# Second batch, first two groups: layer-norm statistics by ScalarE accumulators instead of VectorE batch-norm instructions

## The chip, the cores and the metric

The kernel runs on one core of a Trainium2 chip. The metric is the device time of one launch in microseconds (us). Over three runs the kernel before took 1139.4 us in the median (1138.05 to 1140.47). A core has five engines with a queue each, and each works through its queue strictly in order: PE (TensorE, matmuls), DVE (VectorE), ACT (ScalarE), POOL (GpSimd) and SP (SyncE, which here only starts DMAs). They wait for one another through semaphores.

## The reference, cut to what matters

For 8 batches of 4224 positions with 192 channels the reference computes a dynamic convolution and feeds its output `x` to a Fourier-mixing block with an MLP:

```
w   = softmax(weight_gen)                      # 7 taps, 8 heads
x   = sum over k of w[k] * x_padded[s + k]     # convolution, per head
X   = real(fft over channels(fft over positions(x)))
u   = x + X
mu  = mean(u, axis=-1);  var = mean((u - mu)**2, axis=-1)
un  = (u - mu) / sqrt(var + 1e-6)
out = u + max(un @ w_ch1, 0) @ w_ch2           # 192 -> 768 -> 192
```

The change concerns only how `mu` and `var` are obtained for two pieces of one batch. What is computed stays the same.

## The kernel before, in words

**Tiling.** The 4224 positions of a batch lie as 128 partitions by 33 rows. The rows form nine groups per batch, eight of four rows (128x4x192) and one of a single row; group 1,0 below means batch 1 (the second), group 0. With 8 batches the MLP runs over 72 groups, numbered n = 9b + g.

**Stages of a batch b.**
- `conv(b)`: softmax of the taps on DVE and ACT (L279 to L286), then per group c seven products on DVE (L441), the first into the tile `u`, six into tiles `pr`, which POOL adds to `u` (L450; from batch 2 on all six). A fold on POOL (L464, L466), a first Fourier stage on PE (`pg`, L471), copies on ACT (L476, L478) and sums on DVE (L480, L482) give `gt`, which SP writes to a DRAM buffer `g_d` (L485, L486).
- `transform(b)`: SP reads `g_d` back (L507) in another layout when the whole convolution is done; PE makes the second Fourier stage (`pp`, L517), ACT copies it to `pq` (L521 to L531).
- `mix(b, g)`: third stage on PE (`eo`, L546), an ACT copy (`ot`, L551), four DVE sums into `u` (L552 to L556). `u` is then the input of the norm.
- `norm(b, g)`: statistics, `rs` (row 0: 1/sigma, row 1: the bias -mu/sigma), normalisation on ACT (`un`, L601), a split into two 16-bit halves `hl` (ACT L609, POOL L610 and L612), and a transposing DMA into `ht` (L618).
- `mlp(n)`: PE multiplies `ht` with the first weight in six pieces of five matmuls (`ph`, L643); ACT takes the relu as a 16-bit tile `hh` (L653), DVE the rest that the 16 bits lose (L654, from group 7 on); PE multiplies both with the second weight for the group before (`po`, L666); DVE adds into `u` (L671), SP stores it (L675). `ph` has three buffers, `po` two, the product tiles `pr` five, `un` one.

**Two ways to the statistics.** The flag `quick` in `norm` (L571) chooses. With it, DVE runs four BN_STATS and four BN_AGGR (L580, L581), ACT one square root (L582), DVE the reciprocal (L593) and four small products for the bias (L596). Without it, ACT makes four sums (L586) and four sums of squares (L590) with its accumulator, between them one scaling (L588), then the root (L592); DVE makes the reciprocal (L593), and from batch 1 on POOL the bias in one small product (L599). Before the change `quick` holds for groups 0 to 2 of batch 0 and for groups 0 and 1 of batch 1.

**What sets the order.** `run()` steps generators by due times that are written in units of groups, so that the convolution of batch b+1 runs beside the MLP of batch b. The tile framework then places the instructions of each engine's queue with its own timing model of the whole program (`schedule_with_timeline_sim=True`, L812). So an edit in one place can move instructions everywhere behind it.

Of the kernel before, what the change touches and what calls it, by code (L numbers as in the profile page):

```python
# [30 lines left out]
QUICK = 3  # L31
# [61 lines left out]
def tile_dynconv_fnet_mlp(  # L93
# [20 lines left out]
    NG = 9  # L114
# [6 lines left out]
    def pst(tag, bufs, shape, dt, name):  # L121
        return ps.tile(shape, dt, tag=tag, name=name, bufs=bufs)
# [367 lines left out]
    def keep_warm(bank, nm, lhsT, rhs, count):  # L490

        spare = pst(*bank, [P, 512], F32, f"warm_{nm}")
        for _ in range(count):
            nc.tensor.matmul(spare[:, 0:rhs.shape[-1]], lhsT=lhsT, rhs=rhs, start=True, stop=True)
# [69 lines left out]
    def norm(b, g):  # L564

        T = min(4, N2 - 4 * g)
        u = uv = us[b, g]
        st = sb.tile([P, 4, 2], F32, tag="st", name=f"st_{b}_{g}", bufs=2)
        rs = sb.tile([P, 3, 4], F32, tag="rs", name=f"rs_{b}_{g}", bufs=2)
        junk = sb.tile([P, D], F16, tag="junk", name=f"junk_{b}_{g}", bufs=2)  # L570
        quick = NG * b + g < QUICK or (b == 1 and g < 2)  # L571
        if NG * b + g < QUICK:
            halves = [pst("ph", 3, [P, 2, D], F32, f"un_{b}_{g}_{i}") for i in range(2)]
        else:
            un = sb.tile([P, 4, D], F32, tag="un", name=f"un_{b}_{g}", bufs=1)
            halves = [un[:, 0:2], un[:, 2:4]]
        if quick:
            bn = sb.tile([P, 4, 6], F32, tag="bn", name=f"bn_{b}_{g}", bufs=2)
            for t in range(T):
                nc.vector.bn_stats(out=bn[:, t, :], in_=uv[:, t, :])  # L580
                last_bn[b, g] = nc.vector.bn_aggr(out=st[:, t, :], in_=bn[:, t, :])  # L581
            nc.scalar.activation(rs[:, 0, 0:T], st[:, 0:T, 1], AF.Sqrt, bias=eps_t)  # L582
            neg = -1.0
        else:
            for t in range(T):
                nc.scalar.activation(junk, uv[:, t, :], AF.Identity, accum_out=st[:, t, 0:1])  # L586
            neg = -1.0 / D
            nc.scalar.mul(rs[:, 2, 0:T], st[:, 0:T, 0], neg)  # L588
            for t in range(T):
                nc.scalar.activation(junk, uv[:, t, :], AF.Square, bias=rs[:, 2, t:t + 1],  # L590
                                     accum_out=st[:, t, 1:2])
            nc.scalar.activation(rs[:, 0, 0:T], st[:, 0:T, 1], AF.Sqrt, bias=eps_t, scale=1.0 / D)  # L592
        nc.vector.reciprocal(out=rs[:, 0, 0:T], in_=rs[:, 0, 0:T])  # L593
        if quick or b == 0:
            for t in range(T):
                nc.vector.tensor_scalar(out=rs[:, 1, t:t + 1], in0=st[:, t, 0:1], scalar1=rs[:, 0, t:t + 1],  # L596
                                        scalar2=neg, op0=ALU.mult, op1=ALU.mult)
        else:
            nc.gpsimd.tensor_tensor(out=rs[:, 1, 0:T], in0=rs[:, 2, 0:T], in1=rs[:, 0, 0:T], op=ALU.mult)  # L599
        for t in range(T):  # L600
            nc.scalar.activation(halves[t // 2][:, t % 2, :], uv[:, t, :], AF.Identity,  # L601
                                 bias=rs[:, 1, t:t + 1], scale=rs[:, 0, t:t + 1])
        yield 0.5
        warm = NG * b + g == 0
        hl = sb.tile([P, 4, 2 * D], F16, tag="hl", name=f"hl_{b}_{g}", bufs=2)
        lo_eng = nc.vector if NG * b + g < QUICK else nc.gpsimd
        spans = [(un, 0, T)] if NG * b + g >= QUICK else [(h, 2 * i, 2 * i + 2) for i, h in enumerate(halves)]
        for src, t0, t1 in spans:
            nc.scalar.copy(hl[:, t0:t1, 0:D], src[:, 0:t1 - t0, :])  # L609
            lo_eng.tensor_tensor(out=hl[:, t0:t1, 2 * P:3 * P], in0=src[:, 0:t1 - t0, 0:P],  # L610
                                 in1=hl[:, t0:t1, 0:P], op=ALU.subtract)
            last_lo[NG * b + g] = lo_eng.tensor_tensor(out=hl[:, t0:t1, D:2 * P], in0=src[:, 0:t1 - t0, P:D],  # L612
                                                       in1=hl[:, t0:t1, P:D], op=ALU.subtract)
        if warm:
            keep_warm(("ph", 3), f"hl{g}", hl[:, 0, 0:P], hl[:, T - 1, 0:2 * D], WARM[2])
        hls[NG * b + g] = hl
        ht = sb.tile([P, 4, 3, P], F16, tag="ht", name=f"ht_{b}_{g}", bufs=3)
        nc.sync.dma_start(ht[:, 0:T].rearrange("p t q m -> p (t q) m"),  # L618
                          hl[:, 0:T, :].rearrange("p t d -> p (t d)"), transpose=True)
        state[b, g] = (us.pop((b, g)), ht)  # L620
        yield 2.0
# [110 lines left out]
    for g in range(QUICK):  # L732
        add(0.0, 1.0, behind(last_split[-1].ins, mix(0, g)))
        run()
        add(0.0, 1.0, norm(0, g))
        run()
# [33 lines left out]
    for b in range(B):  # L770
        t0 = NG * b
        pp_at, mix_at, step = (NG - HELD + 0.6, NG - HELD, 0.6) if b == 1 else (PP_AT, 3.0, MIX_STEP)
        if b > 0:
            add(free_at, t0 - pp_at - (CONV_LEAD if b > 1 else 0), next_conv(b) if b > 1 else rest())
            add(t0 - pp_at, t0 - mix_at, transform(b))
            free_at = t0 - pp_at
        for g in range(NG):
            if b > 0 or g >= QUICK:
                at = t0 - mix_at + step * g + (0.7 if b == 0 else 0)
                add(at, at + step, late_mix(g) if b == 0 and g >= QUICK else mix(b, g))  # L780
                add(max(at + step, t0 + g - 2.0), t0 + g - 1.0, norm(b, g))
# [38 lines left out]
```

## Time and profile before

| | |
|---|---|
| median of three runs | 1139.4 us (1138.05 to 1140.47) |
| the profiled execution: its time | 1140.4 us |
| its span, first to last instruction | 1138.5 us, 23781 instructions |
| busy shares of the span | PE 95%, DVE 85%, POOL 76%, ACT 71% |
| granted PE clock | 0.99 on average |

So 1.9 us of the execution's time lie outside the span, and this execution is 1.0 us above the median. A row of a timeline gives start, duration, engine, line, operation and tiles, and in square brackets how long the engine idled before it and for what. Rows of groups give the total busy time and the mean of one in ns. PE overlaps its matmuls: a row of several lasts longer than its share of the queue, so starts are compared with starts.

### The profile page before, as it was taken

The numbers are of one execution on the slowest core, as the hardware profiler recorded it, in microseconds if no ns is written. First come the engines' busy times: TensorE is split into PE (matmuls) and PEld (weight loads), VectorE is DVE, ScalarE is ACT, GpSimd is POOL, SyncE is SP. The second block draws the span as 40 slices with busy tenths as digits, with TensorE's granted clock in tenths as the row PEclk, the third lists the DMA queues.
The fourth block names the chain that finished last, engine by engine and source line by source line (L and its number), as shares of the span: only waits on it lengthen the run. The fifth ranks groups of instructions, "written<-read, shape, count | busy, mean of one in ns | idle before, by whom it ended". The sixth has DMA issues, their size and how long they took to land.

```text
span 1138.5 us, 23781 instructions
## 1 busy us (share of the span) xinstructions
PE 1077.6 (95%) x8476; PEld 816.1 (72%) x8476; DVE 971.3 (85%) x1821; ACT 810.2 (71%) x2522; POOL 867.2 (76%) x745
## 2 busy tenths in 40 slices
PE   5985999998999999999989999999999999999998
PEld 3454677786777867777768867777777867887777
DVE  7988999989989998999988998999899996356443
ACT  4666775456975899569864898668975898579822
POOL 4979598699969998799959998699969998011200
PEclk9996999999999999999999999999999999999999
DMA  8354245514573348415742357415562234422321
GB/s 299 133 150 111 51 115 138 167 39 123 115 205 85 94 115 207 115 50 129 200 117 67 105 106 206 126 39 125 153 144 58 71 73 98 115 56 48 85 46 47
DMA packets 156504, 128.74 MB, mean 113 GB/s; under 512 B 108571, under 2 KB 133088, under 8 KB 156384
## 3 DMA queue, kind: packets, MB, share of 16 engines
q1 hardware_dynamic: 156384, 127.21, 42.1%
q8 instruction: 67, 1.10, 0.4%
q14 instruction: 53, 0.43, 0.1%
HBM read 61.46 MB, written 39.37 MB: 89 GB/s over the span
## 4 chain that ended last, share of the span: by engine, by line
PE 51%; DVE 14%; POOL 11%; ACT 8%; issue 8%; DMA 6%; SPq 1%; POOLq 0%; DVEq 0%; ACTq 0%
PE ph L643 21%; PE po L666 18%; POOL u L450 8%; PE pp L517 5%; DVE pr L441 5%; PE eo L546 2%; DMA g<-g_d 2%; DMA g_d<-gt 2%; PE pa L446 2%; PE pg L471 2%; DVE hh L654 1%; ACT junk L590 1%; DMA ht<-hl 1%; ACT junk L586 1%; ACT hh L653 1%
## 5 line engine op out<-in xcount | busy, mean ns | idle before, releaser
L450 POOL TENSOR_TENSOR u<-u,pr 128x768 f32<-128x768 f32 (+1 forms) x390 | 645.5, 1679 | 63.1 <-DVE pr L441 43.6
L666 PEld LDWEIGHTS <-hh 128*128 128x128 f16 x4248 | 365.1, 99 | 77.2 <-DVE hh L654 5.5
L666 PE MATMUL po<-w2h,hh 128*128 128x192 f16 x2832 | 416.0, 246 | 4.2 <-DVE hh L654 4.1
L643 PE MATMUL ph<-ht,w1h 128*128 128x512 f16 (+1 forms) x1296 | 394.0, 362 | 7.1 <-DMA ht<-hl 3.9
L441 DVE TENSOR_TENSOR pr<-x_sb,wp 128x768 f32<-128x768 f32 (+1 forms) x415 | 354.0, 875 | 17.5 <-POOL u L450 13.3
L666 PE MATMUL po<-w2l,hh 128*128 128x192 f16 x1416 | 345.4, 246 | 0.0
L654 DVE SCALAR_TENSOR_TENSOR hh<-ph,hh 128x512 f16<-128x512 f32 (+1 forms) x390 | 244.8, 634 | 103.2 <-ACT hh L653 101.5
L643 PE MATMUL ph<-ht,w1l 128*128 128x512 f16 (+1 forms) x864 | 309.8, 362 | 0.0
L653 ACT ACTIVATE hh<-ph 128x512 f16<-128x512 f32 (+1 forms) x390 | 213.7, 550 | 129.8 <-PE ph L643 103.6
L643 PEld LDWEIGHTS <-w1h 128*128 128x128 f16 x1296 | 125.5, 98 | 94.7 <-DMA ht<-hl 3.2
L601 ACT ACTIVATE un<-u,rs 128x192 f32<-128x192 f32 x264 | 123.7, 536 | 24.5 <-DVE rs L596 7.9
L610 POOL TENSOR_TENSOR hl<-un,hl 128x512 f16<-128x512 f32 (+1 forms) x69 | 75.6, 1096 | 70.5 <-ACT hl L609 32.4
L643 PEld LDWEIGHTS <-w1l 128*128 128x128 f16 x864 | 85.0, 98 | 52.6 <-issue 4.0
L590 ACT ACTIVATE junk<-u,rs 128x192 f16<-128x192 f32 x244 | 110.6, 453 | 3.2
L586 ACT ACTIVATE junk<-u 128x192 f16<-128x192 f32 x244 | 88.1, 361 | 21.9 <-DVE u L556 19.2
L546 PE MATMUL eo<-cs_sb,pq 97*128 97x97 f32 x544 | 84.5, 273 | 3.5 <-DVE u L556 2.9
L521 ACT COPY pq<-pp 97x204 f32<-97x204 f32 (+1 forms) x96 | 46.7, 488 | 56.9 <-PE pp L517 56.3
L546 PEld LDWEIGHTS eo<-cs_sb,pq 97*128 97x128 f32 x544 | 77.3, 191 | 10.6 <-issue 5.2
L671 DVE SCALAR_TENSOR_TENSOR u<-po,isc,u 128x384 f32<-128x384 f32 (+1 forms) x122 | 72.5, 594 | 8.5 <-PE po L666 8.3
L464 POOL TENSOR_TENSOR sm<-u 128x382 f32<-128x382 f32 x64 | 65.6, 1025 | 5.8 <-DMA g_d<-gt 2.7
L666 PE MATMUL po<-w2f,hh 128*128 128x192 f32 x336 | 62.3, 327 | 0.0
L599 POOL TENSOR_TENSOR rs<-rs 128x4 f32<-128x4 f32 (+1 forms) x61 | 12.8, 213 | 61.5 <-ACT hh L653 37.8
(110 smaller groups left out, 1316.9 us busy)
## 6 DMA issues: line engine op xcount, KB each, us to landing
out_dram<-u SPq DMA_DIRECT2D x64, 384.0 KB
x_sb<-in_x_dram SPq DMA_DIRECT2D x48, 384.0 KB
g<-g_d SPq DMA_DIRECT2D x40, 336.0 KB
x_sb<-in_x_dram SPq DMA_DIRECT2D x8, 864.0 KB
g_d<-gt SPq DMA_DIRECT2D x32, 195.0 KB
g_d<-gt SPq DMA_DIRECT2D x32, 189.0 KB
w<-in_weight_gen_dram SPq DMA_DIRECT2D x6, 924.0 KB
x_sb<-in_x_dram SPq DMA_DIRECT2D x8, 672.0 KB
```

Source lines behind the costliest of these rows:

```text
L441: last_product[b] = nc.vector.tensor_tensor(out=dst, in0=rows, in1=wk, op=ALU.mult)
L450: adder.tensor_tensor(out=u, in0=u, in1=pr, op=ALU.add)
L546: nc.tensor.matmul(eo[:, e, j, :], lhsT=pq[0:DH, e, r, r:r + P], rhs=cs_sb[:, e, :], start=True, stop=True)
L586: nc.scalar.activation(junk, uv[:, t, :], AF.Identity, accum_out=st[:, t, 0:1])
L590: nc.scalar.activation(junk, uv[:, t, :], AF.Square, bias=rs[:, 2, t:t + 1], accum_out=st[:, t, 1:2])
L601: nc.scalar.activation(halves[t // 2][:, t % 2, :], uv[:, t, :], AF.Identity, bias=rs[:, 1, t:t + 1], scale=rs[:, 0, t:t + 1])
L610: lo_eng.tensor_tensor(out=hl[:, t0:t1, 2 * P:3 * P], in0=src[:, 0:t1 - t0, 0:P], in1=hl[:, t0:t1, 0:P], op=ALU.subtract)
L643: last_ph[n] = nc.tensor.matmul(ph[:, 0:T], lhsT=wt[:, cs_], rhs=ht[:, 0:T, blk], start=(i == 0), stop=(i == len(terms) - 1))
L653: nc.scalar.activation(a[:, 0:T], ph[:, 0:T], AF.Relu)
L654: nc.vector.scalar_tensor_tensor(out=l[:, 0:T], in0=ph[:, 0:T], scalar=0.0, in1=a[:, 0:T], op0=ALU.max, op1=ALU.subtract)
L666: nc.tensor.matmul(po[t // 2][:, t % 2, :], lhsT=hx[:, t], rhs=wx[:, c2, :], start=(c2 == 0 and i == 0), stop=(c2 == NH - 1 and i == len(t ...
L671: nc.vector.scalar_tensor_tensor(out=lt, in0=po[t // 2][:, 0:t % 2 + 1], scalar=scales[0][:, 1:2] if f32 else isc, in1=lt, op0=ALU.mult, o ...
```

## The change

One line. The flag no longer holds for groups 0 and 1 of batch 1, so these take the path that all later groups take: eight BN_STATS, eight BN_AGGR and eight L596 leave DVE; ACT gets eight L586, eight L590 and two L588, its two L582 become two L592; POOL gets two L599. The number of matmuls, of DMAs and of loads of ACT's function tables stays.

```diff
--- before
+++ change
@@ -568,7 +568,7 @@
         st = sb.tile([P, 4, 2], F32, tag="st", name=f"st_{b}_{g}", bufs=2)
         rs = sb.tile([P, 3, 4], F32, tag="rs", name=f"rs_{b}_{g}", bufs=2)
         junk = sb.tile([P, D], F16, tag="junk", name=f"junk_{b}_{g}", bufs=2)
-        quick = NG * b + g < QUICK or (b == 1 and g < 2)
+        quick = NG * b + g < QUICK
         if NG * b + g < QUICK:
             halves = [pst("ph", 3, [P, 2, D], F32, f"un_{b}_{g}_{i}") for i in range(2)]
         else:
```

Up to these statistics the queues are the same; behind them all five engines' queues are reordered. In the rows below the batch is left out of a tile's name: `hh_7_3` is piece 3 of group 7 (here of batch 0), `u_0` group 0 (here of batch 1), and the last number counts tiles. An "x4" stands for four in a row.

DVE's queue at the statistics of group 1,0, before:

```order
L580 BN_STATS bn_0_2377<-u_0_830 128x6 x4
L654 SCALAR_TENSOR_TENSOR hh_7_3_2369<-ph_7_3_2360,hh_7_3_2369 128x512
L441 TENSOR_TENSOR pr_3_3_2735<-x_sb,wp_2109 128x768
L581 BN_AGGR st_0_2373<-bn_0_2377 128x2 x3
L552 TENSOR_TENSOR eo_1_2396<-eo_1_2396,ot_1_2431 128x2x97
L581 BN_AGGR st_0_2373<-bn_0_2377 128x2
L441 TENSOR_TENSOR pr_3_4_2745<-x_sb,wp_2109 128x768
L654 SCALAR_TENSOR_TENSOR hh_7_4_2412<-ph_7_4_2405,hh_7_4_2412 128x512
L654 SCALAR_TENSOR_TENSOR hh_7_5_2444<-ph_7_5_2429,hh_7_5_2444 128x512
L553 TENSOR_TENSOR eo_1_2396<-eo_1_2396,ot_1_2431 128x194
L441 TENSOR_TENSOR pr_3_5_2767<-x_sb,wp_2109 128x768
L593 RECIPROCAL rs_0_2374<-rs_0_2374 128x4
```

and with the change:

```order
L654 SCALAR_TENSOR_TENSOR hh_7_3_2369<-ph_7_3_2360,hh_7_3_2369 128x512
L441 TENSOR_TENSOR pr_3_3_2729<-x_sb,wp_2109 128x768
L552 TENSOR_TENSOR eo_1_2393<-eo_1_2393,ot_1_2428 128x2x97
L441 TENSOR_TENSOR pr_3_4_2739<-x_sb,wp_2109 128x768
L553 TENSOR_TENSOR eo_1_2393<-eo_1_2393,ot_1_2428 128x194
L654 SCALAR_TENSOR_TENSOR hh_7_4_2409<-ph_7_4_2402,hh_7_4_2409 128x512
L593 RECIPROCAL rs_0_2374<-rs_0_2374 128x4
L654 SCALAR_TENSOR_TENSOR hh_7_5_2441<-ph_7_5_2426,hh_7_5_2441 128x512
L555 TENSOR_TENSOR u_1_853<-u_1_853,eo_1_2393 128x4x97
L556 TENSOR_TENSOR u_1_853<-u_1_853,eo_1_2393 128x4x95
```

The batch-norm rows are gone, the reciprocal of group 1,0 stands between two L654, and the sums that finish `u_1` (L555, L556) follow at once; before, five rows stood between the reciprocal and them. On ACT the four L601 of group 1,0 now stand behind four L586 and the L588 of group 1,1.

POOL's queue around the first low halves of batch 1, before:

```order
L450 TENSOR_TENSOR u_3_2701<-u_3_2701,pr_3_3_2735 128x768
L450 TENSOR_TENSOR u_3_2701<-u_3_2701,pr_3_4_2745 128x768
L450 TENSOR_TENSOR u_3_2701<-u_3_2701,pr_3_5_2767 128x768
L610 TENSOR_TENSOR hl_0_2422<-un_0_2376,hl_0_2422 128x4x128
L612 TENSOR_TENSOR hl_0_2422<-un_0_2376,hl_0_2422 128x4x64
L450 TENSOR_TENSOR u_3_2701<-u_3_2701,pr_3_6_2787 128x768
```

and with the change:

```order
L599 TENSOR_TENSOR rs_0_2374<-rs_0_2374 128x4
L464 TENSOR_TENSOR sm_2_2637<-u_2_2483 128x2x191
L466 TENSOR_TENSOR sm_2_2637<-u_2_2483 128x2
L450 TENSOR_TENSOR u_3_2695<-u_3_2695,pr_3_3_2729 128x768
L450 TENSOR_TENSOR u_3_2695<-u_3_2695,pr_3_4_2739 128x768
L610 TENSOR_TENSOR hl_0_2419<-un_0_2376,hl_0_2419 128x4x128
L612 TENSOR_TENSOR hl_0_2419<-un_0_2376,hl_0_2419 128x4x64
```

One L450 fewer stands ahead of L610, and the new L599 ahead of the fold. The second group's L610 and L612 come, with the change, behind five L450, a fold and an L599, counted from those of the first group; before, behind eight L450 and a fold.

ACT's queue at the start of transform 2, before:

```order
L653 ACTIVATE hh_5_1_3771<-ph_5_1_3763 128x512
L653 ACTIVATE hh_5_2_3810<-ph_5_2_3799 128x512
L521 COPY pq<-pp_0_0_3640 97x12x17
L526 COPY pq<-pp_0_0_3640 97x11x17
L531 COPY pq<-pp_0_0_3640 97x12x17
```

and with the change:

```order
L653 ACTIVATE hh_5_3_3853<-ph_5_3_3832 128x512
L653 ACTIVATE hh_5_4_3897<-ph_5_4_3871 128x512
L521 COPY pq<-pp_0_0_3634 97x12x17
L526 COPY pq<-pp_0_0_3634 97x11x17
L531 COPY pq<-pp_0_0_3634 97x12x17
```

Two more MLP pieces are done ahead of the transform. On PE, counted over the whole queue, so many more matmuls stand ahead of the first L517: 10 L643 and 30 L666 at transform 2, then 10 and 39, 6 and 19, 1 and 13, 1 and 5, 3 and 1 at transforms 3 to 7. On DVE, between the last product of a convolution and the first `pr` product of the next, there stood 7, 8, 9, 8 and 7 L654 and 3, 2, 3, 3 and 3 L671 behind convolutions 2 to 6; with the change 6, 7, 8, 8 and 8 L654 and 2, 2, 3, 3 and 3 L671.

## The prediction

> **What bounds the kernel.** I read the page's busy shares first, then the waits of PE, then the timelines where these waits lie. PE is busy 95% of the span, so only its idle time can be won, and lateness of another engine counts only where PE comes to wait for it. In the waits of PE over the whole program, rows give the total, the number and the longest:
>
> ```profile
> PE 1077.6 (95%) x8476; PEld 816.1 (72%) x8476; DVE 971.3 (85%) x1821; ACT 810.2 (71%) x2522; POOL 867.2 (76%) x745
> PE pp L517 <- DMA g<-g_d: 13.8, 7, 3.3
> PE po L666 <- DVE hh L654: 4.1, 4, 1.6
> PE ph L643 <- DMA ht<-hl: 3.9, 4, 2.2
> ```
>
> All four waits for L654 and two of those for `ht` stand where the change acts. PE's timeline from 258 to 290 us:
>
> ```profile
> 264.90 0.34 PE L666 MATMUL po<-w2h,hh 128*128 128x192 f16 x2 [1.63 <-DVE hh L654]
> 267.11 0.38 PE L643 MATMUL ph<-ht,w1h 128*128 128x512 f16 x1 [1.22 <-DMA ht<-hl]
> 278.69 0.34 PE L666 MATMUL po<-w2h,hh 128*128 128x192 f16 x2 [0.88 <-DVE hh L654]
> 280.15 0.34 PE L666 MATMUL po<-w2h,hh 128*128 128x192 f16 x2 [0.79 <-DVE hh L654]
> 281.61 0.34 PE L666 MATMUL po<-w2h,hh 128*128 128x192 f16 x2 [0.79 <-DVE hh L654]
> 284.73 0.38 PE L643 MATMUL ph<-ht,w1h 128*128 128x512 f16 x1 [0.29 <-DMA ht<-hl]
> ```
>
> That is 5.6 us of PE time, behind a DVE that carries the batch-norm work. The stretches there and after (columns: length, then PE, PE loads, DVE, ACT, POOL busy):
>
> ```profile
> 240.00:270.00 30.00, 27.08 (x227) 22.78 (x226) 29.77 (x73) 11.25 (x30) 28.94 (x23) 1.00 0.22 60
> 270.00:300.00 30.00, 27.25 (x209) 19.69 (x208) 29.76 (x61) 29.21 (x108) 29.77 (x23) 1.00 0.44 116
> ```
>
> DVE and POOL are full in both, ACT is idle for 18.75 us of the first and full in the second.
>
> **What is removed, added and moved.** DVE, timeline:
>
> ```profile
> 248.56 1.13 DVE L580 BATCH_NORM_STATS2 bn<-u 128x6 f32<-128x192 f32 x4
> 249.61 0.67 DVE L654 SCALAR_TENSOR_TENSOR hh<-ph,hh 128x512 f16<-128x512 f32 x1
> 251.06 0.31 DVE L581 BATCH_NORM_AGGREGATE st<-bn 128x2 f32<-128x6 f32 x3
> 257.44 0.54 DVE L556 TENSOR_TENSOR u<-u,eo 128x380 f32<-128x380 f32 x1
> 258.10 0.56 DVE L596 TENSOR_SCALAR rs<-st,rs 128x1 f32<-128x1 f32 x4
> ```
>
> Four BN_STATS hold the queue 1.05 us (248.56 to 249.61), four BN_AGGR about 0.3, four L596 about 0.5: 1.85 us per group, 3.7 us for two. ACT and POOL get, by rows of the same operations on later groups:
>
> ```profile
> 280.90 0.20 ACT L588 ACTIVATE rs<-st 128x4 f32<-128x4 f32 x1
> 281.14 0.46 ACT L590 ACTIVATE junk<-u,rs 128x192 f16<-128x192 f32 x1
> 281.72 0.46 ACT L590 ACTIVATE junk<-u,rs 128x192 f16<-128x192 f32 x1
> L586 ACT ACTIVATE junk<-u 128x192 f16<-128x192 f32 x244 | 88.1, 361 | 21.9 <-DVE u L556 19.2
> L599 POOL TENSOR_TENSOR rs<-rs 128x4 f32<-128x4 f32 (+1 forms) x61 | 12.8, 213 | 61.5 <-ACT hh L653 37.8 <-DVE rs L593 20.5 <-ACT junk L590 3.0
> ```
>
> An L590 with its accumulator read takes 0.58 us start to start; an L586, 0.09 us shorter by the two means (361 against 453 ns), 0.49; L588 0.24. A group costs ACT 4 x 0.49 + 0.24 + 4 x 0.58 = 4.5 us, both 9 us. The 18.75 us of idle ACT cover them; without that cover they would cost what ACT's full next stretch shows, up to 9 us. POOL gets 2 x 0.21 = 0.4 us. The root, its table load and the reciprocal stay.
>
> **The first group, followed by hand.** `u` of group 1,0 is ready at 245.5:
>
> ```profile
> 244.99 0.54 DVE L556 TENSOR_TENSOR u<-u,eo 128x380 f32<-128x380 f32 x1
> 245.40 0.60 ACT L653 ACTIVATE hh<-ph 128x512 f16<-128x512 f32 x1 [1.78 <-PE ph L643]
> 251.68 1.28 ACT L582 ACT_TABLE_LOAD   x1
> 252.97 0.30 ACT L582 ACTIVATE rs<-st,eps_t 128x4 f32<-128x4 f32 x1
> 258.39 0.99 ACT L601 ACTIVATE un<-u,rs 128x192 f32<-128x192 f32 x2 [2.29 <-DVE rs L596]
> 261.59 1.16 POOL L610 TENSOR_TENSOR hl<-un,hl 128x512 f16<-128x512 f32 x1 [0.82 <-ACT hl L609]
> 263.34 3.59 POOL L450 TENSOR_TENSOR u<-u,pr 128x768 f32<-128x768 f32 x2
> 279.16 1.16 POOL L610 TENSOR_TENSOR hl<-un,hl 128x512 f16<-128x512 f32 x1
> ```
>
> From 246.0 the ACT statistics with an `ot` between them end at 250.7, an L653 and the table load follow, the root ends near 252.8. Behind this root now wait the reciprocal on DVE and, in its queue, the last L654 of group 7 and L555 and L556 of group 1,1. DVE so idles about 1 us, yet `u_1` is done near 255.0 instead of 258.0 (before, its L556 starts at 257.44), since the batch-norm and two products no longer stand ahead. ACT makes the sums of group 1,1 first, normalises group 1,0 from about 257.4 and casts it by 260.9, where POOL's L610 before starts at 261.59; `ht` is half a microsecond earlier. The second group gains more: its low halves stand behind five L450 at 1.8 us (3.59 for two), a fold and an L599 after those of the first, not eight and a fold, so L610 starts near 273.4, not 279.16, and the wait at 284.73 is gone.
>
> For PE, products no longer pile up ahead of the last three L654 of group 1,0: I place the third at 278.8, where PE, without its earlier waits, asks for it at 278.5. Of 5.6 us I keep 2.6 (1.3 for the last pieces of group 8, whose L654 now come one by one, 0.5 for `ht`, 0.8 for the last piece of group 1,0). **PE gains 3.0 us by 285.** The bounds are 0, if the late L653 of groups 7 and 1,0 on ACT eat it, and 5.6.
>
> **POOL pays.** One add fewer ahead of L610 leaves POOL idle from 259.0 to 260.9, 1.1 us more than the 0.82 before; with 0.4 for L599 the convolution of batch 2 is **1.5 us later**. Bounds: 0.4 and 1.8 us more (one add).
>
> **What the transforms give back.** Behind this place PE's largest waits are those for `g_d`:
>
> ```profile
> 343.81 0.94 PE L517 MATMUL pp<-te_sb,g 102*97 102x102 f32 x8 [1.82 <-DMA g<-g_d]
> 594.53 0.94 PE L517 MATMUL pp<-te_sb,g 102*97 102x102 f32 x8 [3.35 <-DMA g<-g_d]
> 853.80 0.91 PE L517 MATMUL pp<-te_sb,g 102*97 102x102 f32 x8 [1.20 <-DMA g<-g_d]
> 322.49 2.09 DVE L279 TENSOR_REDUCE wp<-w 128x264 f32<-128x1848 f32 x1
> 340.16 9.43 POOL L450 TENSOR_TENSOR u<-u,pr 128x768 f32<-128x768 f32 x5 [7.81 <-DVE pr L441]
> ```
>
> A wait for `g_d` becomes: before, plus what PE is early, plus what the convolution is late, less the PE work newly put ahead of L517. That work is 10 x 0.215 + 30 x 0.082 = 4.6 us at transform 2 (starts of neighbouring rows; the 2.06 us of a piece twice and a little), and by the counts of matmuls 5.4, 2.8, 1.3, 0.6 and 0.7 at the later ones. At transform 2: 1.82 + 3.0 + 1.5 - 4.6 = 1.7, the gain stands. But the shift fades: at transform 6 (853.80) PE waits in both orders, so its lead cannot be more than 0.6 us less the lateness of convolution 6. That lateness changes at the seams, where POOL idles 7.81 us for DVE's softmax: the L654 (0.6 us each) and L671 (0.53) put there are fewer by 1.1, 0.6 and 0.6 us behind convolutions 2 to 4, and equal behind 5. The convolution then is 1.5 - 2.3 = 0.8 us early, and PE ahead by 0.6 + 0.8 = 1.4. A part of the later small waits (2.16 us for one `ht` among the 3.9 of the row above) falls otherwise in a new order, either way; I add 0.4 of gain for the earlier `ht`. **The sum: 1.8 us faster**, 1140.4 - 1.8 = 1138.6 in the profiled execution; with the median 1.0 below it, 1137.6 us.
>
> **The clock.** The wait of 3.35 us cost more than its length, by PE's timeline behind it:
>
> ```profile
> 589.70 0.38 PE L643 MATMUL ph<-ht,w1h 128*128 128x512 f16 x1
> 589.91 0.38 PE L643 MATMUL ph<-ht,w1l 128*128 128x512 f16 x1
> 596.38 0.63 PE L643 MATMUL ph<-ht,w1l 128*128 128x512 f16 x1
> 596.81 1.06 PE L643 MATMUL ph<-ht,w1h 128*128 128x512 f16 x2
> 580.00:600.00 20.00, 16.55 (x127) 11.63 (x125) 17.56 (x27) 10.52 (x22) 9.38 (x8) 0.91 0.51 132
> ```
>
> L643 goes from 0.21 to 0.43 us start to start and the granted clock of the stretch is 0.91. The 0.09 that lack are 1.8 us of 20. [...]
>
> **The rivals.**
> - *The gain is kept.* If convolutions come 2 us or more early (a seam's DVE work can fall otherwise by several L654), the wait at 594.53 falls to 3.35 + 3.0 - 2.0 - 2.8 = 1.55, and the half clock goes with it. Gain 3.0 + 1.8 and the shorter waits 0.4: 5.2 us, 1134.2. For it: DVE, full at 240 to 300, is what is relieved. Against: POOL is full too and gets more.
> - *Slower: the convolution stays late.* If the seams give nothing back, the 1.5 us stay, and at 594.53 the wait is 3.35 + 3.0 + 1.5 - 2.8 = 5.05 us; the lead at transform 6 is 0.6 - 1.5, a loss of 0.9. If one more wait (343.81 has 1.82) passes 3.35 on the way behind transform 6, 1.8 us of half clock add to it: 2.7 us slower, 1142.1. It decides from a lateness of 0.6 us at transform 6. For it: POOL does not idle between 265 and 330, so nothing there makes up for it. Against: the fewer L654 at three seams.
> - *All given back.* PE's 3 us arrive and the waits for `g_d` take them: 1139.4, no change.
> - *ACT becomes the bound.* Nine microseconds on an engine that is full from 280 on: against it stands the idle time up to 268, and the two groups finish before the full stretch begins. I give it no number of its own beyond the lower bound of the gain.
>
> **How the numbers follow.** Forecast (1.8 us faster, own range 1135.9 to 1139.4) 0.45; gain kept 0.20; slower 0.23; all given back 0.12. A difference under 0.2%, 2.3 us, cannot be told from no change, so the line lies at 1137.1 and 1141.7. Below the first lie the gain kept and 0.19 of the forecast: faster 0.39. Slower keeps 0.22 beyond 1141.7. Same: 0.39. The range reaches from 1133.6, where the gain kept is nearly whole, to 1143.4, the slower case with another microsecond from a late seam.
>
> **What would show it.** No L580 behind 110 us; the four waits for L654 near 265 to 282 down to at most two, together under 2.6 us; L610 of the second group near 273; POOL's wait ahead of its first L610 near 1.9 us; L517 of transform 2 waiting 1 to 3 us. The prediction is wrong in its first half if PE still waits over 4 us between 258 and 290, and in its second if convolutions 5 and 6 end over 2 us off their old times (L517 of transform 6 waits to 853.80 before) or if the granted clock dips elsewhere than at transform 4.

## The result: slower, and the profile after

Over 12 executions each, taken in turn on the same chips, the changed kernel takes 1145.6 us in the median (1142.7 to 1149.5) and the kernel before 1140.0 (1136.7 to 1143.6). The ratio is 1.0052 with a 95% interval of 1.0035 to 1.0069: 0.5% slower, 5.6 us by the two medians, and 2.2 us above the upper end of the predicted range (1143.4). The profiled execution of the changed kernel took 1148.2 us with a span of 1146.5.

The page's busy shares and PE's waits in the changed kernel:

```profile
PE 1086.2 (95%) x8476; PEld 820.2 (72%) x8476; DVE 969.1 (85%) x1797; ACT 818.3 (71%) x2556; POOL 866.8 (76%) x747
PE pp L517 <- DMA g<-g_d: 16.5, 8, 3.4
PE ph L643 <- DMA ht<-hl: 5.3, 5, 3.0
PE po L666 <- DVE hh L654: 1.4, 3, 0.6
```

The four waits of L666 for L654 that stood before 290 us (4.1 us) are gone, as the change should make them; the 1.4 us of the last row lie behind 380, and no wait of PE over 0.7 us is left between 240 and 290. The waits for `g_d` and for `ht` grew, by 2.7 and 1.4 us. Their two longest, from PE's timeline:

```profile
410.97 0.38 PE L643 MATMUL ph<-ht,w1h 128*128 128x512 f16 x1 [3.03 <-DMA ht<-hl]
478.23 0.50 PE L517 MATMUL pp<-te_sb,g 102*97 102x102 f32 x3 [3.36 <-DMA g<-g_d]
```

The first stands where PE asks for `ht` of group 2,1, the second group of the third batch, 130 us behind the change; before, PE waited 0.07 us there. The second is the first L517 of transform 3, where it waited 1.16.

**Where the time went.** The comparison is by equal work: the times at which PE of either kernel has done the same amount of it (the sum of each matmul's own start-to-start time). The changed kernel is 3.1 us behind before the change acts at all. The stretches show why (length, then PE, PE loads, DVE, ACT, POOL busy, granted clock); before:

```profile
100.00:120.00 20.00, 8.67 (x41) 4.73 (x41) 19.86 (x68) 14.04 (x28) 19.84 (x14) 0.66 0.27 40
220.00:240.00 20.00, 17.27 (x134) 14.70 (x135) 13.62 (x18) 11.92 (x32) 19.92 (x13) 1.00 0.36 101
400.00:420.00 20.00, 19.70 (x142) 13.06 (x141) 19.58 (x36) 18.84 (x62) 20.00 (x19) 1.00 0.35 87
```

and changed:

```profile
100.00:120.00 20.00, 10.16 (x32) 4.92 (x32) 19.61 (x67) 13.38 (x26) 19.84 (x14) 0.50 0.29 40
220.00:240.00 20.00, 16.64 (x120) 13.90 (x119) 13.55 (x18) 11.35 (x31) 19.84 (x13) 0.91 0.40 113
400.00:420.00 20.00, 16.48 (x105) 10.27 (x105) 16.26 (x28) 16.59 (x56) 18.09 (x15) 0.91 0.44 95
```

In this one execution the clock was lower at 100 to 120 and at 220 to 240 us, where the queues of both kernels are still the same, so the 3.1 us are not the change's. From 260 to 290 PE gains 4.7 us and is 1.6 us ahead. Between 400 and 420 it loses 5.3, the wait of 3.03 and half clock behind it (0.91), at transform 3 another 1.7, and with smaller gains and losses behind it is 7.6 us late at the end. From 260 on that is 4.5 us lost, near the 5.6 between the medians.

### The profile page after: what moved, and what is told of

It reads as the page before. It is cut to its first block, busy times and chain, and to the rows that moved or that the text cites. A ratio compares the mean times of both kernels' runs of the same rounds, so it can differ in the third digit from the quotient of the medians.

```text
span 1146.5 us, 23767 instructions
## 1 busy us (share of the span) xinstructions
PE 1086.2 (95%) x8476; PEld 820.2 (72%) x8476; DVE 969.1 (85%) x1797; ACT 818.3 (71%) x2556; POOL 866.8 (76%) x747
## 4 chain that ended last, share of the span: by engine, by line
PE 53%; DVE 14%; ACT 11%; POOL 7%; DMA 7%; issue 6%; SPq 1%; DVEq 0%; POOLq 0%; ACTq 0%
PE ph L643 22%; PE po L666 18%; PE pp L517 5%; POOL u L450 5%; DVE pr L441 5%; ACT junk L590 3%; PE eo L546 2%; DMA g<-g_d 2%; ACT junk L586 2%; DMA g_d<-gt 2%; PE pg L471 2%; PE pa L446 2%; DMA ht<-hl 1%; ACT hh L653 1%; DVE hh L654 1%
## 5 line engine op out<-in xcount | busy, mean ns | idle before, releaser
L450 POOL TENSOR_TENSOR u<-u,pr 128x768 f32<-128x768 f32 (+1 forms) x390 | 644.4, 1672 | 76.2 <-DVE pr L441 54.7
L666 PEld LDWEIGHTS <-hh 128*128 128x128 f16 x4248 | 364.1, 98 | 78.5 <-DVE hh L654 3.6
L666 PE MATMUL po<-w2h,hh 128*128 128x192 f16 x2832 | 414.4, 246 | 2.0 <-DVE hh L654 1.4
L643 PE MATMUL ph<-ht,w1h 128*128 128x512 f16 (+1 forms) x1296 | 397.3, 364 | 7.7 <-DMA ht<-hl 5.3
L666 PE MATMUL po<-w2l,hh 128*128 128x192 f16 x1416 | 346.8, 246 | 0.0
L654 DVE SCALAR_TENSOR_TENSOR hh<-ph,hh 128x512 f16<-128x512 f32 (+1 forms) x390 | 245.9, 637 | 112.5 <-ACT hh L653 111.5
L643 PE MATMUL ph<-ht,w1l 128*128 128x512 f16 (+1 forms) x864 | 312.3, 364 | 0.0
L643 PEld LDWEIGHTS <-w1h 128*128 128x128 f16 x1296 | 126.5, 99 | 92.0 <-issue 3.0
L601 ACT ACTIVATE un<-u,rs 128x192 f32<-128x192 f32 x264 | 123.7, 534 | 18.3 <-DVE rs L596 5.1
L643 PEld LDWEIGHTS <-w1l 128*128 128x128 f16 x864 | 85.6, 99 | 57.1 <-issue 9.4
L610 POOL TENSOR_TENSOR hl<-un,hl 128x512 f16<-128x512 f32 (+1 forms) x69 | 75.0, 1087 | 56.8 <-ACT hl L609 24.1
L590 ACT ACTIVATE junk<-u,rs 128x192 f16<-128x192 f32 x252 | 114.0, 453 | 4.2
L586 ACT ACTIVATE junk<-u 128x192 f16<-128x192 f32 x252 | 90.8, 360 | 28.4 <-DVE u L556 24.6
L671 DVE SCALAR_TENSOR_TENSOR u<-po,isc,u 128x384 f32<-128x384 f32 (+1 forms) x122 | 72.8, 597 | 10.0 <-PE po L666 9.6
L464 POOL TENSOR_TENSOR sm<-u 128x382 f32<-128x382 f32 x64 | 65.3, 1020 | 5.8 <-DMA g_d<-gt 2.8
L599 POOL TENSOR_TENSOR rs<-rs 128x4 f32<-128x4 f32 (+1 forms) x63 | 12.7, 203 | 72.4 <-DVE rs L593 70.2
L666 PE MATMUL po<-w2f,hh 128*128 128x192 f32 x336 | 63.3, 331 | 0.0
```

The lines of the kernel that those rows point to most:

```text
L450: adder.tensor_tensor(out=u, in0=u, in1=pr, op=ALU.add)
L643: last_ph[n] = nc.tensor.matmul(ph[:, 0:T], lhsT=wt[:, cs_], rhs=ht[:, 0:T, blk], start=(i == 0), stop=(i == len(terms) - 1))
L654: nc.vector.scalar_tensor_tensor(out=l[:, 0:T], in0=ph[:, 0:T], scalar=0.0, in1=a[:, 0:T], op0=ALU.max, op1=ALU.subtract)
L666: nc.tensor.matmul(po[t // 2][:, t % 2, :], lhsT=hx[:, t], rhs=wx[:, c2, :], start=(c2 == 0 and i == 0), stop=(c2 == NH - 1 and i == len(t ...
L671: nc.vector.scalar_tensor_tensor(out=lt, in0=po[t // 2][:, 0:t % 2 + 1], scalar=scales[0][:, 1:2] if f32 else isc, in1=lt, op0=ALU.mult, o ...
```

## The experiments

Three theories were open. ORDER: the edit lets the scheduler lay out the queues anew, and that order costs the time, wherever the statistics are made. LOAD: the 9 us more on ACT and POOL's lateness cost it, in any order. LEAD: PE arrives early at group 2,1 and only collects there what it had won.

To hold an order, most of these kernels carry a table with the place of every instruction in its engine's queue. Once the program is traced, an edge that fixes the order of issue, and waits for nothing, is drawn from each instruction to the one before it:

```diff
+    last = {}
+    for k in order:
+        i = made[int(k)]
+        if i.engine in last:
+            tc.add_manual_dep(i, last[i.engine], mybir.DependencyInfo(mybir.DependencyClass.NoSync,
+                              mybir.DependencyReason.DATA), reason="order")
+        last[i.engine] = i.name
```

With the table a single row of one queue can be moved while all else stays. Every ratio below is against the kernel before, run on the same chip beside it, and rests on 12 executions where no other number is given; changes of the table are given in words. Waits and timelines are of one execution each. "POOL's cycle 3" is the time from the end of the last small L450 (128x192, the single row) of convolution 2 to that of convolution 3: 121.5 us before and 128.9 in the changed kernel. It scatters between executions by some us: with the same rows up to there it took 132.0 in another kernel below.

### Whose order: the statistics or the queues

The first kernel has the changed instructions, in the changed order up to the first L517 of transform 2 and in the order of before behind it.

```diff
-order = order of the changed kernel
+order = changed, for all that the kernel before issues ahead of L517 of transform 2; then as before
```

> Instructions of the changed kernel; queues in the changed kernel's order up to the first L517 of transform 2, behind it in the order of the kernel before (held by a table that orders issue only). Theory ORDER (the loss comes from the new order behind the place): PE gains about 4.5 us of waits between 258 and 290 as in the changed kernel, gives them back at L517 of transform 2 (wait 1.8 + 4.5 = about 6.3 us, since nothing new stands ahead), the POOL cycle of convolution 3 (last small L450 to last small L450) is back at 121 to 123 us, and the time is 1138 to 1142. Theory LOAD (the 9 us more on ACT and the POOL lateness cost, whatever the order): cycle 3 stays near 129 us and the time is 1144 to 1147. Theory LEAD (the stall at L643 of group 2,1 comes only because PE arrives early there): as ORDER, with no wait over 1 us at that L643.

Measured: ratio 0.9997 (0.9973 to 1.0022). By equal work PE gains 4.8 us between 260 and 290, waits 6.43 us at transform 2, and shows no wait for `ht` of group 2,1. POOL's cycle 3 is 121.8 us. PE's timeline at transform 2:

```profile
343.31 0.97 PE L517 MATMUL pp<-te_sb,g 102*97 102x102 f32 x4 [6.43 <-DMA g<-g_d]
```

The second kernel is its mirror: nothing is changed in the statistics, and the changed kernel's order begins at transform 2.

```diff
-order = order of the kernel before
+order = as before, for all that the changed kernel issues ahead of L517 of transform 2; then changed
```

> Instructions of the kernel before (batch-norm statistics on DVE); queues in the order of before up to the first L517 of transform 2 as the changed kernel places it, behind it in the changed kernel's order. ORDER: slower than before although nothing is changed in the statistics, 1143 to 1147, POOL cycle 3 at 127 us or more. LOAD: no change, 1138 to 1141, cycle 3 near 121.5. LEAD: PE is late by the 4.7 us that it did not gain, so the wait of 3.0 us at L643 of group 2,1 is under 0.5, POOL cycle 3 is 123 to 125 (the low halves of one more group stand ahead of the convolution's end, 1.8 us), and the time is 1139 to 1142.

Measured, over 5 executions: ratio 1.0080 (1.0057 to 1.0103), as slow as the changed kernel or slower, with POOL's cycle 3 at 133.0 us. PE's timeline:

```profile
415.10 0.58 PE L643 MATMUL ph<-ht,w1h 128*128 128x512 f16 x1 [3.11 <-DMA ht<-hl]
```

ORDER holds. LOAD falls: the added work is in the first kernel and costs nothing, and it is not in the second, which is slow. LEAD falls too: here PE comes to group 2,1 4.1 us later than in the changed kernel and waits 3.11 us all the same. So the wait is no collecting of a lead; something on the way to `ht` moves along with PE.

### Which queue: a transposing DMA behind two stores

SP's timeline ahead of that `ht`, with the sum on DVE (L482) that the stores send, and the L643 that uses it; before:

```profile
397.08 0.34 DVE L482 TENSOR_TENSOR gt<-pg,up 128x190 f32<-128x190 f32 x1
397.71 0.36 SPq L485 DMA_DIRECT2D g_d<-gt  x1
398.11 0.31 SPq L486 DMA_DIRECT2D g_d<-gt  x1
398.52 0.59 SPq L675 DMA_DIRECT2D out_dram<-u  x1
404.40 2.01 SPq L618 DMA_TRANSPOSE ht<-hl  x1
408.16 0.39 PE L643 MATMUL ph<-ht,w1h 128*128 128x512 f16 x1
```

and changed, with the low halves on POOL (L612) that L618 sends as well:

```profile
403.74 0.68 POOL L612 TENSOR_TENSOR hl<-un,hl 128x256 f16<-128x256 f32 x1
404.60 0.35 DVE L482 TENSOR_TENSOR gt<-pg,up 128x190 f32<-128x190 f32 x1
405.01 0.33 SPq L485 DMA_DIRECT2D g_d<-gt  x1
405.39 0.31 SPq L486 DMA_DIRECT2D g_d<-gt  x1
405.80 2.03 SPq L618 DMA_TRANSPOSE ht<-hl  x1
```

In both kernels the stores stand ahead of L618. Before, they had gone 6 us ahead of it. In the changed kernel L482 comes at 404.60 instead of 397.08, so SP stands at the stores while `hl` is ready at 404.42, and L618 goes 1.4 us late. It also takes longer: 5.17 us from issue to the first L643 (405.80 to 410.97) against 3.76 (404.40 to 408.16), with 384 KB of stores just ahead. PE asks at 407.94, only 0.15 us earlier than before, so nearly all of the 3.03 us are these two, 1.4 each. That the stores make the way longer is my reading of the two durations; with L618 ahead of them it takes 3.70 us (the next kernel). `gt` itself hangs on a matmul of PE (L471), a copy on ACT and two sums on DVE, so a late PE makes the stores late too. The second kernel above shows it: its L471 starts at 404.46 instead of 400.41, its L482 at 408.66 instead of 404.60 and its L618 at 409.85 instead of 405.80, all 4.05 us later, as PE is, and the wait is as long.

The third kernel is the changed one with one row of SP moved.

```diff
+L618 DMA_TRANSPOSE ht_2_1
 L485 DMA g_d<-gt
 L486 DMA g_d<-gt
-L618 DMA_TRANSPOSE ht_2_1
```

> The changed kernel in its own order, but on SP the transposing DMA of group 2,1 (L618) stands ahead of the two stores L485 and L486 of the convolution. If SP's queue makes the stall: L618 issues at about 404.4 instead of 405.8 and lands without the stores beside it, the wait of 3.03 us at that L643 falls to 0.2 to 1.6 us, no half clock follows it, POOL cycle 3 falls from 128.9 by 2 us or more, and the time is 1141 to 1144. If the stall only collects PE's lead and costs nothing behind it: the wait falls as said, cycle 3 stays within 1 us of 128.9 and the time within 1.5 us of the changed kernel's (1144 to 1147).

Measured: ratio 1.0006 (0.9990 to 1.0022), from 1.0052: this one row carries 0.46% of 1140 us, 5.2 us, nearly the whole loss (the intervals leave 0.23% either way). PE waits 0.21 us there, without half clock (granted clock 1.00 from 400 to 420 us), the transfer takes 3.70 us from issue to PE, and POOL's cycle 3 is 124.4 us, 4.5 less than in the changed kernel's profile. SP's and PE's timelines:

```profile
401.52 1.44 SPq L618 DMA_TRANSPOSE ht<-hl  x1
403.06 0.79 SPq L485 DMA_DIRECT2D g_d<-gt  x1
405.22 0.38 PE L643 MATMUL ph<-ht,w1h 128*128 128x512 f16 x1 [0.21 <-DMA ht<-hl]
```

**Why 3 us of waiting cost 5.** On PE itself the sum is short: 3.03 us of wait, and half clock behind it (0.91 of 20 us, 1.8 us). PE would get part of that back at transform 3, by a shorter wait there, if the convolution stayed on time. It does not, for the stall runs on through the queues:

```profile
412.51 0.60 ACT L653 ACTIVATE hh<-ph 128x512 f16<-128x512 f32 x1 [1.91 <-PE ph L643]
413.14 0.69 DVE L654 SCALAR_TENSOR_TENSOR hh<-ph,hh 128x512 f16<-128x512 f32 x1 [2.28 <-ACT hh L653]
415.27 0.69 DVE L654 SCALAR_TENSOR_TENSOR hh<-ph,hh 128x512 f16<-128x512 f32 x1 [1.14 <-ACT hh L653]
417.77 1.82 POOL L450 TENSOR_TENSOR u<-u,pr 128x768 f32<-128x768 f32 x1 [1.49 <-DVE pr L441]
420.84 0.20 POOL L599 TENSOR_TENSOR rs<-rs 128x4 f32<-128x4 f32 x1 [1.25 <-DVE rs L593]
```

PE has no product for ACT, ACT no `hh` for DVE, DVE stands at L654 with the convolution's products behind it, and POOL runs dry. Of the 7.4 us that cycle 3 grew, 5.4 are idle time of POOL (9.35 to 14.78 us) and 1.8 the low halves of one more group, put ahead of the convolution's end. Convolution 3 is late with PE, and transform 3 gives nothing back: PE waits 3.36 us there. Most of that wait is not the stall's, though, for with the row moved PE still waits 2.76 us at transform 3 (1.16 before), with half clock behind it (0.83 at 460 to 480 us).

### Half the change

```diff
-        quick = NG * b + g < QUICK or (b == 1 and g < 2)
+        quick = NG * b + g < QUICK or (b == 1 and g == 1)
```

> The change for group 1,0 alone (group 1,1 keeps the batch-norm statistics); the scheduler makes its own order, which behind the place is nearly that of the changed kernel: on SP the transposing DMA of group 2,1 stands again behind x loads, a store of the output and the convolution's two stores L485 and L486. ORDER: the stall of about 3 us at L643 of group 2,1 is there, POOL cycle 3 is 127 to 131 us, and the time is 1143 to 1147 although half of the added ACT work is left out. LOAD (the time goes with the 9 us on ACT): half of the loss, 1141.5 to 1144, cycle 3 near 125.

Measured: ratio 1.0022 (0.9997 to 1.0048), 1144.4 us; wait at group 2,1 2.11 us with half clock (0.83 at 400 to 420 us), POOL's cycle 3 129.8. The stall and the cycle come as ORDER says; the time alone does not tell the theories apart, nor a loss from none.

```diff
-        quick = NG * b + g < QUICK or (b == 1 and g < 2)
+        quick = NG * b + g < QUICK or (b == 1 and g == 0)
```

> The change for group 1,1 alone; here the scheduler's own order is a third one, in which on SP the stores L485 and L486 also stand just ahead of the transposing DMA of group 2,1, with one output store fewer between. ORDER: the time follows the wait at that L643: over 2 us there, then 1143 to 1146; under 1 us, then 1138 to 1141.5. LOAD: as for the other half, 1141.5 to 1144 whatever that wait is.

Measured: ratio 1.0014 (0.9990 to 1.0037), 1143.6 us; no wait at group 2,1, cycle 3 122.8. This is a miss: with that wait gone I expected at most 1141.5. It is a small one, for the kernel before took 1141.7 us on that chip and the interval includes no change. The order has stalls of its own. PE's timeline:

```profile
853.10 0.42 PE L517 MATMUL pp<-te_sb,g 102*97 102x102 f32 x2 [3.69 <-DMA g<-g_d]
```

and one of 3.41 us for L471 at 273.7, both with half clock behind them (0.91 at 840 to 860 us, 0.83 at 260 to 280); by equal work this kernel gains nothing between 260 and 290. So one L643 does not foretell the time of an order.

### The convolution's end

Three kernels tried to bring the end of a convolution forward. The first moves the low halves of group 2,7 behind the last adds of convolution 3.

```diff
-L610, L612 hl_2_7
 L450 u_3_8
-L599 rs_2_8
 L450 u_3_8
+L610, L612 hl_2_7
+L599 rs_2_8
```

> The changed kernel in its own order, but on POOL the low halves L610 and L612 of group 2,7 and the L599 of group 2,8 stand behind the last two adds of convolution 3, as in the kernel before. If these 1.8 us set convolution 3's end: POOL cycle 3 falls from 128.9 to about 127.1, the wait of 3.36 us at L517 of transform 3 to about 1.6, and the time by 1.5 to 2 us to 1143 to 1144.5 (by up to 3.5 where a half clock goes with the wait). If POOL has idle time there anyway: cycle 3 within 0.5 us of 128.9 and no change, 1145 to 1146.5.

Measured, over 9 executions: ratio 1.0052 (1.0030 to 1.0075), nothing won, although cycle 3 is 127.0 us, as expected (within its scatter). From the start of the last small L450 to the first L507 it now takes 14.6 us instead of 12.4, since the last two pairs of stores begin 9.1 us after the fold L464 of group 7, which stands ahead of the moved rows, in this kernel as in the changed one; the last add does not set them. The next two do it at the end of convolutions 2 to 7, with L601, L609 and L618 of the groups concerned moved back, in the changed order (with the swap on SP) and in that of before.

```diff
-L610, L612 hl of groups 6 and 7
 L450, the last add of convolutions 2 to 7
+L610, L612 hl of groups 6 and 7
```

> The changed kernel in its own order with the SP swap, and at the end of convolutions 2 to 7 the low halves L610 and L612 of groups 6 and 7 of the running batch stand behind the convolution's last add on POOL (with L601 and L609 of groups 7 and 8 on ACT and the transposing DMAs on SP moved back to fit); nothing but the order differs. If the end of the convolution on POOL is what sets each L517: the last small L450 comes 1.8 us (3.6 in convolutions 2 and 3) earlier, the waits for g_d at transforms 2 to 7, 10.8 us in the swapped kernel, fall to 1 to 4, and the time is 1130 to 1136. If something else ends the waits (DVE's products, the DMAs of g_d): the waits fall by under 3 us in all and the time is 1138 to 1142.

Measured, over 11 executions: ratio 1.0065 (1.0042 to 1.0088), worse than the single swap's 1.0006. My own order had put the fault in again. SP's timeline at transform 2, where convolution 2 ended at 329.9 us on POOL:

```profile
338.25 1.44 SPq L618 DMA_TRANSPOSE ht<-hl  x1
339.79 0.82 SPq L485 DMA_DIRECT2D g_d<-gt  x1
```

The convolution's last stores stand behind a transposing DMA whose low halves I had moved back, and transform 2 waits 4.48 us instead of 1.61.

> The kernel before in its own order with the same move of the low halves behind the ends of convolutions 2 to 7. If the convolution's end on POOL sets each L517: waits for g_d at transforms 2 to 6, 8.9 us before, fall to 1 to 4, and the time is 1131 to 1136; with the changed kernel's version 2 to 4 us below it, PE's gain at the changed groups is worth something once the transforms no longer take it back; with both within 1.5 us, it is worth nothing. If something else ends the waits: 1138 to 1141.

Measured: ratio 0.9983 (0.9961 to 1.0005), which cannot be told from no change; the waits for `g_d` at transforms 3 and 4 are under 0.8 us, those at 2, 5, 6 and 7 stay at 1 to 2. (At transform 4 it was 3.35 us.) The 1131 to 1136 us that the first theory asks for did not come.

### SP's queue mended

One more single row: L618 of group 2,7 from between the last stores of convolution 3 to behind the third L507.

```diff
 L485, L486 g_d<-gt
-L618 DMA_TRANSPOSE ht_2_7
 L485, L486 g_d<-gt
 L507 g<-g_d x3
+L618 DMA_TRANSPOSE ht_2_7
```

> The changed kernel in its own order; only the transposing DMA of group 2,7 on SP is moved, from between the last two pairs of stores of convolution 3 to behind the third load L507 of transform 3, where it stands in the kernel before. If it holds up the transform: the 12.4 us from the last small L450 of convolution 3 to the first L507 fall to about 11, the wait of 3.36 us at transform 3 by 1 to 2, and the time by 1 to 3 us to 1142.5 to 1144.5 against 1140 before. If the DMAs of g_d are bound by the stores alone: no change, 1145 to 1147.

Measured: ratio 1.0028 (1.0008 to 1.0047). Its interval overlaps the changed kernel's, and the 12.4 us from the last add to L507 are 12.3 now: the last stores then wait for `gt` as long as they had waited for the transposing DMA (they go at 469.76 instead of 470.08). So that row did not hold the transform up, and where the difference comes from stays open. This is the kernel whose cycle 3 took 132.0 us: the same stall, 3.10 us, had 6.8 us of half clock around it instead of 3.4.

The last three edit SP's rows alone, where the trace shows a transposing DMA late while PE is about to ask for it, or one between a convolution's last stores and the first load of the transform. The changed kernel:

```diff
+L618 ht_2_1 ahead of L485, L486
+L618 ht_4_1, ht_5_1, ht_6_1 ahead of the L675 before them
+L618 ht_2_7, ht_3_7, ht_4_7, ht_5_7 behind the third L507
```

> The changed kernel in its own order, and only SP's queue is edited: group 2,1's transposing DMA ahead of the stores (as in the run before), those of groups 4,1, 5,1 and 6,1 ahead of the output store that they stand behind, and those of groups 2,7 to 5,7 behind the third L507 of the next transform. If SP's queue is what the change spoiled: the waits at L643 of 4,1 and 5,1 (0.5 and 1.4 us with the single swap) go, the waits for g_d at transforms 3 to 6 (8.5 us) fall by 3 to 6, and the time is 1.5 to 4 us below the single swap's, at 0.997 to 1.000 of the kernel before. If compute queues set the transforms: within 1 us of the single swap, 1.000 to 1.002.

Measured: ratio 0.9951 (0.9930 to 0.9972), 1136.1 us. It beats both kernels, by 1.0% the changed one, and lies below the 0.997 to 1.000 that I had expected, which its interval just reaches. The wait for `ht` of 5,1 (1.38 us with the single swap) is gone, that of 4,1 fell from 0.48 us to 0.30, and POOL's cycles 5 to 7 are 125.3 to 125.5 us (127.0 to 128.0 in the changed kernel). The waits for `g_d` at transforms 3 to 6 fell by 2.4 us against the single swap, less than expected; in the two profiled executions the clock was also up, 0.989 in the mean against 0.985. Over all executions the means are 0.986 both, so what makes the rest of the 0.55% is not shown. That it beats the kernel before with SP mended (0.9967, below) is not shown: the intervals overlap.

The kernel before:

```diff
+L618 ht_4_1, ht_5_1, ht_6_1 ahead of L485, L486
+L618 ht_1_7 behind the third L507
```

> The kernel before in its own order, only SP's queue edited: the transposing DMAs of groups 4,1, 5,1 and 6,1 ahead of the convolution's stores, that of group 1,7 behind the third L507 of transform 2. If stores ahead of a transposing DMA cost PE there too: the wait of 2.16 us at L643 of group 5,1 falls under 0.5, the wait at transform 2 (1.82) by 1 us or more, and the time is 0.997 to 0.999 of before. If that wait is the norm's lateness: unchanged, 0.999 to 1.001.

Measured: ratio 0.9967 (0.9949 to 0.9985), 1136.6 us. The wait of 2.16 us at group 5,1 is gone, and that at transform 2 fell from 1.82 us to 0.70: from the end of the last small L450 to the first L507 it took 8.5 us there instead of 9.8, so here the row between the last stores did hold the transform up, if one execution of each can tell. SP's and PE's timelines before:

```profile
785.11 0.31 SPq L486 DMA_DIRECT2D g_d<-gt  x1
785.52 2.00 SPq L618 DMA_TRANSPOSE ht<-hl  x1
792.12 0.39 PE L643 MATMUL ph<-ht,w1h 128*128 128x512 f16 x1 [2.16 <-DMA ht<-hl]
```

and with the row moved:

```profile
782.16 1.40 SPq L618 DMA_TRANSPOSE ht<-hl  x1
783.67 0.84 SPq L485 DMA_DIRECT2D g_d<-gt  x1
787.30 0.38 PE L643 MATMUL ph<-ht,w1h 128*128 128x512 f16 x1
```

Behind the stores it took 6.6 us from issue to PE (785.52 to 792.12). Ahead of them it is issued 3.4 us earlier, and PE finds `ht` there at 787.30.

> The changed instructions with the changed order up to transform 2 and the order of before behind it, and the transposing DMAs of groups 4,1, 5,1 and 6,1 ahead of the stores on SP. The wait of about 6.4 us at transform 2 stays (the lead of 4.7 us is lost there whatever stands on SP later); the waits of 1.0 and 2.1 us at L643 of 4,1 and 5,1 fall under 0.5 each. If the lead is worth nothing once the transform takes it: within 1 us of the kernel before with the same edits. If it is worth something: 2 us or more below that kernel.

Measured: ratio 0.9990 (0.9974 to 1.0006). Waits for `ht` of 4,1 and 5,1 are gone, that of 6.33 us at transform 2 stays. (The fourth edit of the kernel before has no place here: group 1,7's transposing DMA goes ahead of the stores already.) It is no faster than the kernel before with the same edits (0.9967), rather 2.2 us slower by the medians, which the intervals do not settle: the lead of 4.5 us in this execution is lost at transform 2, and then it is worth nothing.

| instructions | order of before | changed order | SP mended, before | SP mended, changed |
|---|---|---|---|---|
| of before | 1 | 1.0080 | 0.9967 | |
| changed | 0.9997 | 1.0052 | 0.9990 | 0.9951 |

(The first row's 1.0080 and the second row's 0.9997 and 0.9990 are mixed: each keeps its own order up to transform 2 and takes the column's behind it.) Down a column the statistics, with the order up to transform 2, make 0.3% or less, which the intervals do not tell from nothing. Along a row the order makes 1.1% (0.9967 to 1.0080) and 1.0% (0.9951 to 1.0052) from the best to the worst.

## Why the prediction was wrong

- **DVE relieved, ACT's work hidden.** Right in kind. ACT grew by 8.1 us (810.2 to 818.3; 9 said). DVE fell by 2.2 us, not 3.7. ACT's idle time took the work in: with the order of before behind transform 2 it costs nothing that the interval shows (0.9973 to 1.0022).
- **PE gains 3.0 us by 285.** The place was right, the term was sized too small: 4.7 us, and 4.8 in the run with the order of before. I had kept 2.6 us of the waits; all four for L654 are gone, and so are those for `ht`.
- **POOL pays 1.5 us.** Not borne out, though the changed kernel's profile seems to bear it out: POOL's idle time ahead of the first L610 is 2.43 us (1.9 said), and cycle 2, from convolution 1 to convolution 2, is 124.5 us instead of 123.1. That is luck. Half clock followed the wait at transform 1 there (0.91 at 220 to 240 us). The single swap has the same queues up to transform 2, and in its execution the clock stayed up; the first row is the changed kernel's, the others are the swap's:

```profile
263.35 1.16 POOL L610 TENSOR_TENSOR hl<-un,hl 128x512 f16<-128x512 f32 x1 [2.43 <-ACT hl L609]
260.51 1.16 POOL L610 TENSOR_TENSOR hl<-un,hl 128x512 f16<-128x512 f32 x1 [1.15 <-ACT hl L609]
220.00:240.00 20.00, 16.94 (x132) 14.42 (x133) 13.95 (x18) 11.59 (x32) 19.86 (x13) 1.00 0.40 106
```

  In the four profiles with this order up to transform 2 and full clock there, the idle time is 0.77 to 1.15 us and cycle 2 122.8 to 123.0: convolution 2 is not late. In the mirror kernel, which keeps the old statistics and had half clock there (0.91), they are 2.20 and 124.3. The term should have been about nothing: L610 starts at 259.5 to 260.5 in the four, where I had set 260.9.
- **Transform 2.** The rule for the wait held, its agreement with the number is luck: 1.7 us said, 1.60 measured, since PE's gain was 1.7 us larger than said and the convolution 1.5 us less late:

```profile
346.57 0.65 PE L517 MATMUL pp<-te_sb,g 102*97 102x102 f32 x5 [1.60 <-DMA g<-g_d]
```

  With the measured terms it gives 1.82 + 4.7 - 4.6 = 1.9 us, and the profiles of this order show 1.6 to 1.9. Without the 4.6 us of work newly ahead of L517 the same lead waited 6.43 us.
- **The later transforms: the step that failed.** I took the later waits for `ht` to fall "otherwise in a new order, either way" and added 0.4 us of gain, and I had the convolutions 3 to 5 come earlier by the fewer L654 at their seams. In place of that gain one `ht` behind two stores on SP cost 5.2 us, by the run that moves its row, and convolution 3 took 7.4 us longer. I had followed POOL, DVE and PE past the change and not SP, the queue on which `ht` travels. It could have been seen without a run. On SP the stores stand directly ahead of L618 of group 2,1, and what they send comes later in each queue in the changed order: L482 20 rows behind that group's reciprocal on DVE instead of 8, its copies 24 rows behind the group's root on ACT instead of 8 (accumulator reads not counted), its fold 4 rows ahead of L610 on POOL instead of 10.
- **The rivals.** "Slower" had the right sign, but as another mechanism: a convolution 2 that stays late, and it was not late by the change. What came was a wait on a DMA queue that no rival named. The condition of "gain kept", half clock gone at transform 4, did not arise there (2.40 us of wait, half clock behind it, 0.91). That a wait brings half clock once it passes 3.35 us, as the rivals count it, no run shows: in the changed kernel's profile it came behind 2.40 us and not behind 3.36 (the last section has the others).
- **The range** ended at 1143.4. It covered one more dip of the clock, not a stall of 3 us with the lateness that it hands on.

## What to carry to other kernels

When a scheduler lays out the queues from its own timing, an edit is two edits: what it does, and the order that comes out. Judge them apart, by holding the order, before calling the idea good or bad; here the idea is worth 0.3% or less, which could not be told from nothing, and the order 1%. Follow every queue that the critical data travels on, the one that only issues DMAs as well: here a transfer that was ready but stood behind another that waited for its data cost its own lateness (1.4 us), a longer way to PE (5.17 us instead of 3.76) and what the stalled engine handed on; moving four rows of such a queue made the kernel before 0.3% faster, eight rows the changed one 1%.

## What the runs showed of the hardware

**Half clock came behind shorter waits than the one that I had seen.** These are the waits of PE over 1 us behind 125 us in the profiled executions of the two kernels, by the granted clock of the 20 us from the end of each (length of the wait in us, in brackets the end):

| | 0.91 behind it | 1.00 behind it |
|---|---|---|
| before | 3.35 (594.53) | 1.16 (466.58), 1.20 (853.80), 1.22 (267.11), 1.39 (723.24), 1.63 (264.90), 1.82 (343.81), 2.16 (792.12), 2.55 (221.75) |
| changed | 1.80 (857.53), 2.33 (223.18), 2.40 (602.59), 3.03 (410.97) | 1.06 (797.19), 1.60 (346.57), 1.92 (730.68), 3.36 (478.23) |

The wait at transform 4 in the changed kernel,

```profile
602.59 1.36 PE L517 MATMUL pp<-te_sb,g 102*97 102x102 f32 x8 [2.40 <-DMA g<-g_d]
```

is followed by a stretch (600 to 620 us) at 0.91, and the 3.36 us at 478.23 by one at 1.00 (480 to 500). So the length of a wait does not settle it in these two executions: 1.80 us had half clock behind it, 2.55 and 3.36 us had none. Nor do the queues ahead of it: at transform 1, where they are still the same in both kernels, 2.33 us were followed by 0.91 and 2.55 by 1.00. What settles it these profiles do not show. A stretch of 20 us at 0.91 lacks 1.8 us of full clock, as much as the shortest wait of the five.

**It is also most of the scatter.** The changed kernel's 12 executions run from 1142.7 us at a mean granted clock of 0.988 to 1149.5 at 0.979, and a straight line through them falls by 0.87 us per 0.001 of clock (correlation -0.96; -0.58 to -0.94 in the kernels of the experiments). One execution tells little of a change of 0.5%.
